# Attention and gated feed-forward on one core: a score product's weight in the merge of two row halves, N/1.2 to N/0.6

## The chip, the cores and the metric

The kernel runs on one NeuronCore of a Trainium2 chip. The metric is the device time of one execution in microseconds, the median of several runs.

## The reference

Attention with a decay term for 8 x 8 heads (sequence 576, head size 64), then a feed-forward block on the 4608 tokens, all in float32:

```python
scores = q @ k.T / 8                      # per head, 576 x 576
cum = cumsum(log(clip(f, 1e-4, 1)))
scores = where(causal, -1e9, scores + cum[:, None] - cum[None, :])
attn = softmax(scores)                    # rows
x = (attn @ v), heads side by side        # 4608 x 512
h = x @ w_in                              # 512 x 2048
out = (h * erf(softplus(h))) @ w_out      # 2048 x 512
```

## The kernel before

There are two stages. In the first, attention, heads are taken in pairs: head 0 of a pair lies in partitions 0 to 63 of the tiles q and k, head 1 in partitions 64 to 127. A matmul that contracts over 64 partitions uses one half of TensorE's rows, so products of head 0 (row half 0) and of head 1 (row half 1) can run side by side. From about 300 us on follows the feed-forward stage (class Moe: line 186 the up products, line 249 the down products), which uses all 128 rows and lies outside the change.

Attention is a loop over steps t = 0 to 67. Two steps make a pair of heads: an even step takes the row blocks 4 and 1, an odd one 3, 2 and 0 (BLOCKS), and the causal width of each block sets the columns of its product (PARTS): 256, 320 and 192 in an even step, 448, 320 and 64 in an odd one, the block of 576 being cut in two. [...] A step t writes, in this order:

- row_halves(t, t - 3): TensorE's score products of step t into two PSUM banks s (one for each head, line 707, and the mask matmuls on the diagonal, line 713), merged with the transposes of step t - 3's probabilities (line 736, into PSUM tiles yz, x and a part of o)
- evacuate(t - 3, 2): ScalarE copies yz (line 799)
- values(t - 4): TensorE's products with v (line 825), over all 128 rows
- run_jobs(t): pieces of weight preparation on VectorE, ScalarE and GpSimd, spread over the steps by a credit for each step
- reduce(t, 0) on VectorE (line 762: adds the decay and takes the extreme, frees the bank of head 0), exps(t, 0) on ScalarE (line 774), invert(t - 1) (reciprocal, VectorE, line 781), normalize(t - 1) on GpSimd (line 788), then reduce(t, 1) and exps(t, 1) for head 1
- evacuate(t - 3) of x and of the part of o on VectorE (line 797), store(t - 4) on VectorE (lines 834 to 838)

Each of the two s banks is used again in the next step, so a product of step t + 1 waits for the reduction of step t of the same head. A transpose in step t waits for normalize of step t - 3, and for the copies that free its PSUM tile.

row_halves merges two lists. List 0 (row half 0) has head 0's products, its masks, and then ten transposes. List 1 (row half 1) has twelve or thirteen transposes first, and then head 1's products and masks. Each item has a cost; each list has a clock. The next item is taken from list 1 if its clock is behind that of list 0, otherwise from list 0, and its cost is added to that list's clock. The costs are 61 for a transpose, 28 for a mask matmul, and for a product of N columns N/1.2. The costs serve only to order the instructions. Steps 1 and 2 list the two halves one after the other (apart=True), step 0 and the steps after 63 have only one kind of work. A product in float32 runs as two passes, each with its own weight load, so it shows as two records.

Of the kernel before, what the change touches and what calls it, by code (L numbers as in the profile page):

```python
# [40 lines left out]
PARTS = [[(512, 4, 320, 576), (192, 4, 0, 320), (0, 1, 0, 192)], [(0, 3, 0, 448), (512, 2, 0, 320), (448, 0, 0, 64)]]  # L41
# [342 lines left out]
def attention_moe(ctx, tc, q2, k2, vp, f, w_in, w_out, out):  # L384
# [283 lines left out]
    with ExitStack() as ph:  # L668
# [31 lines left out]
        def score_work(t):  # L700


            p, half = divmod(t, 2)
            q, k = pairs[p][:2]
            s = [ps_s.tile([P, 1024], F32, name=f"s{t}_{j}", tag="s") for j in range(2)]
            def product(j, at, i, k0, k1):
                nc.tensor.matmul(out=s[j][:, at:at + k1 - k0], lhsT=q[HALF[j], PAD + START[i]:PAD + END[i]],  # L707
                                 rhs=k[HALF[j], k0:k1], start=at in (0, 192, 512) and i != 1, stop=False,
                                 skip_group_check=True)

            def edge(j, i, c):
                to = SCOL[i] + START[i] + 64 * c
                nc.tensor.matmul(out=s[j][:, to:to + 64], lhsT=above[HALF[j], c], rhs=keys[HALF[j]],  # L713
                                 start=False, stop=bool(c), skip_group_check=True)

            raw_scores[t] = s
            probs[t] = wk.tile([P, TCOLS[half]], F32, name=f"pr{t}", tag=f"pr{half}")
            stats[t] = wk.tile([P, 3, 2, len(BLOCKS[half])], F32, name=f"st{t}", tag=f"st{half}")
            return [[((part[3] - part[2]) / 1.2, lambda j=j, part=part: product(j, *part)) for part in PARTS[half]]
                    + [(28, lambda j=j, i=i, c=c: edge(j, i, c)) for i in BLOCKS[half] for c in range(not i, 2)]  # L720
                    for j in range(2)]

# [18 lines left out]
        def row_halves(t, turned=None, apart=False):  # L741

            scored = score_work(t) if t < NH else [[], []]
            moved = [[], []] if turned is None else transpose_work(turned)
            work, clock = [scored[0] + moved[0], moved[1] + scored[1]], [0, 0]
            while any(work):
                h = int(not work[0] or not apart and work[1] and clock[1] < clock[0])
                time, do = work[h].pop(0)
                clock[h] += time
                do()  # L750
# [172 lines left out]
        for t in range(3, NH + 4):  # L923
            p, half = divmod(t, 2)
# [101 lines left out]
```

## Time and profile before

| | before |
|---|---|
| median of 3 runs | 1072.78 us (1072.72 to 1072.9) |
| the profiled execution | 1072.71 us |
| its span, first to last instruction | 1070.8 us |
| granted TensorE clock | 1.000 |
| TensorE busy | 1063.5 us (99%) |
| VectorE, ScalarE, GpSimd busy | 725.4, 779.6, 508.2 us |
| HBM read and written | 113.41 and 39.99 MB |

The busy time of an engine counts any time in which at least one of its instructions runs. PE is TensorE's matmuls, PEld its weight loads, DVE VectorE, ACT ScalarE, POOL GpSimd. Lines in order of time give start and duration in us, engine, line, operation, output and inputs, shape and count; consecutive instructions of the same line are merged into one row under the first one's shape. Ends of matmuls are modelled and include the way through the array, so durations of following matmuls overlap: the distance of starts is the rate.

### The profile page before, as it was taken

To read this page: it belongs to the slowest core of one execution; us is meant where nothing else is said; L and a number is where in the kernel's file an instruction comes from. 1 tells how busy PE (TensorE), PEld (TensorE's weight loads), DVE (VectorE), ACT (ScalarE), POOL (GpSimd) and SP (SyncE) were. 2 spreads that over 40 slices of the span, in tenths; PEclk is the share of its full clock that TensorE was granted. 3 is DMA by queue.
4 is the path that set the end of the run, shared out by engine and by line. 5 is a ranking of instruction groups with operands and counts; after the bars stand their busy time and mean duration, and the time that the engine had idled before them with its cause. 6 is when DMAs were issued, how large, how long until landed. Compare 5 with 4: busy or idle time off the path is not lost.

```text
span 1070.8 us, 22986 instructions
## 1 busy us (share of the span) xinstructions
PE 1063.5 (99%) x8490; PEld 949.9 (89%) x8490; DVE 725.4 (68%) x1701; ACT 779.6 (73%) x1732; POOL 508.2 (47%) x650
## 2 busy tenths in 40 slices
PE   9999999999999999999999999999999999999998
PEld 7888888888898889989999999988988988898996
DVE  6888888988767986776878755646555455655532
ACT  7888888889867787777787776668565665856653
POOL 4578989878534535452633532233143143323313
PEclk9999999999999999999999999999999999999999
DMA  7678887666623152441516154451302213130021
GB/s 267 216 245 267 295 271 267 222 222 222 218 79 132 38 203 84 143 162 61 187 58 219 67 194 190 169 195 55 123 11 79 89 59 118 45 133 1 25 94 59
DMA packets 70366, 154.88 MB, mean 145 GB/s; under 512 B 6960, under 2 KB 19504, under 8 KB 69232
## 3 DMA queue, kind: packets, MB, share of 16 engines
q1 hardware_dynamic: 70256, 153.43, 41.1%
q8 instruction: 67, 1.10, 0.4%
q14 instruction: 43, 0.35, 0.1%
HBM read 113.41 MB, written 39.99 MB: 143 GB/s over the span
## 4 chain that ended last, share of the span: by engine, by line
PE 94%; DVE 3%; ACT 2%; issue 1%; DMA 0%; POOL 0%; DVEq 0%; ACTq 0%; POOLq 0%
PE y L249 35%; PE m L186 31%; PE s L707 11%; PE o L825 9%; PE yz L736 3%; PE x L736 3%; PE s L713 1%; DVE x L127 1%; DVE e L220 0%; ACT L217 0%; ACT e L217 0%; PE o L736 0%; ACT e L214 0%; DMA fr<-in_f_dram 0%; DVE h L210 0%
## 5 line engine op out<-in xcount | busy, mean ns | idle before, releaser
L230 POOL TENSOR_TENSOR gl<-e,gh 128x384 fp32r<-128x384 f32 x192 | 227.0, 1212 | 388.6 <-ACT gh L229 388.6
L186 PE MATMUL m<-x,wi 128*128 128x384 f32 x2016 | 385.6, 337 | 1.0 <-DVE h L210 0.6
L186 PEld LDWEIGHTS m<-x,wi 128*128 128x128 f32 x2016 | 357.3, 188 | 18.9 <-DVE h L210 2.5
L249 PE MATMUL y<-wo,gh 128*128 128x512 f32 x1152 | 359.4, 393 | 0.0
L249 PEld LDWEIGHTS y<-wo,gh 128*128 128x128 f32 x1152 | 214.6, 188 | 34.4
L249 PE MATMUL y<-wo,gl 128*128 128x512 f32 x576 | 227.1, 394 | 0.0
L788 POOL TENSOR_SCALAR pr<-pr,st 128x576 f32<-128x576 f32 (+4 forms) x320 | 173.9, 565 | 67.9 <-DVE st L781 53.5
L707 PE MATMUL s<-k,q 64*128 64x320 f32 (+4 forms) x768 | 195.5, 405 | 0.6 <-PE s L713 0.6
L774 ACT ACTIVATE pr<-pr,st 128x576 f32<-128x576 f32 (+3 forms) x320 | 176.0, 552 | 19.5 <-DVE st L762 16.9
L762 DVE CUSTOM_DVE_ANT_0 pr<-s,c 128x576 f32<-128x576 f32 (+3 forms) x320 | 140.4, 483 | 43.6 <-PE x L736 24.4
L707 PEld LDWEIGHTS s<-k,q 64*128 64x128 f32 x768 | 127.9, 188 | 27.1 <-issue 0.9
L220 DVE TENSOR_TENSOR e<-e,h 128x384 f32<-128x384 f32 x192 | 114.7, 646 | 24.1 <-ACT e L217 24.1
L249 PEld LDWEIGHTS y<-wo,gl 128*128 128x128 f32 x576 | 108.1, 188 | 24.5
L199 ACT COPY sa<-m 128x384 f32<-128x384 f32 x48 | 23.0, 479 | 141.4 <-PE m L186 141.3
L214 ACT ACTIVATE e<-h 128x384 f32<-128x384 f32 x192 | 92.6, 521 | 30.7 <-DVE h L210 22.2
L202 DVE TENSOR_TENSOR sb<-m,sa 128x384 f32<-128x384 f32 x48 | 26.7, 557 | 121.8 <-PE m L186 61.8
L229 ACT CAST gh<-e 128x384 fp32r<-128x384 f32 x192 | 87.9, 511 | 24.7 <-DVE e L220 23.5
L825 PE MATMUL o<-pt,v 128*64 128x128 f32 (+1 forms) x1920 | 102.5, 259 | 0.0
L825 PEld LDWEIGHTS o<-pt,v 128*64 128x64 f32 x1920 | 93.7, 137 | 3.5 <-issue 0.2
L127 DVE TENSOR_TENSOR x<-t,x 128x768 fp32r<-128x768 f32 x77 | 83.8, 1105 | 15.3 <-ACT x L122 15.3
L217 ACT ACTIVATE e<-e 128x384 f32<-128x384 f32 x192 | 84.9, 513 | 0.5
L210 DVE TENSOR_TENSOR h<-m,sb 128x384 f32<-128x384 f32 x96 | 53.1, 553 | 45.8 <-PE m L186 45.8
(112 smaller groups left out, 1237.5 us busy)
## 6 DMA issues: line engine op xcount, KB each, us to landing
v<-in_vp_dram SPq DMA_DIRECT2D x32, 576.0 KB, 4.6
c<-cum_d SPq DMA_DIRECT2D x60, 288.0 KB, 5.9
t<-xt_d SPq DMA_DIRECT2D x44, 384.0 KB, 5.5
q<-in_q_dram SPq DMA_DIRECT2D x32, 320.0 KB, 5.0
k<-in_k_dram SPq DMA_DIRECT2D x32, 288.0 KB, 5.3
xt_d<-xo SPq DMA_DIRECT2D x32, 288.0 KB, 2.3
part_d<-yo SPq DMA_DIRECT2D x36, 256.0 KB, 2.8
yo<-part_d SPq DMA_DIRECT2D x36, 256.0 KB, 4.3
```

The lines of the kernel that those rows point to most:

```text
L127: eng.tensor_tensor(out=x[:, 1, kd], in0=self.src[r][:, kd], in1=x[:, 0, kd].bitcast(F32), op=ALU.subtract)
L186: nc.tensor.matmul(out=ps, lhsT=w[:, wp, ws], rhs=x[:, xp, kd], start=first and kd == 0 and j == 0, stop=kd == 1 and j == 2 and i in (1, 2 ...
L214: self.nc.scalar.activation(out=e, in_=self.h[n, q], func=AF.Softplus)
L220: self.nc.vector.tensor_mul(self.e[n, q], self.e[n, q], self.h.pop((n, q)))
L229: nc.scalar.copy(out=gh, in_=e)
L230: nc.gpsimd.tensor_tensor(out=gl, in0=e, in1=gh.bitcast(F32), op=ALU.subtract)
L249: yield nc.tensor.matmul(out=y[tb], lhsT=g[:, cs], rhs=w[:, f, wp], start=first, stop=last)
L707: nc.tensor.matmul(out=s[j][:, at:at + k1 - k0], lhsT=q[HALF[j], PAD + START[i]:PAD + END[i]], rhs=k[HALF[j], k0:k1], start=at in (0, 192, ...
L762: nc.vector.tensor_tensor_reduce(out=to[:, ::-1] if j else to, in0=score, in1=decay_, scale=-0.125, scalar=BIG, op0=ALU.add, op1=ALU.min, ...
L774: nc.scalar.activation(out=seg, in_=seg, func=AF.Exp, bias=st[:, 0, j, m:m + 1], scale=-1.0, accum_out=st[:, 1, j, m:m + 1])
L788: nc.gpsimd.tensor_scalar(out=seg, in0=seg, scalar1=st[:, 2, j, m:m + 1], scalar2=1.0, op0=ALU.mult, op1=ALU.mult)
L825: nc.tensor.matmul(out=o[h, to:to + 64 * (1 + (a < b))], lhsT=v[:, ch, h], rhs=src, start=m == 0, stop=m == len(parts) - 1, skip_group_che ...
```

## The change

The cost of a score product in the merge goes from N/1.2 to N/0.6. Transposes and masks keep theirs. No instruction is added, removed or altered; the order of TensorE's instructions within row_halves follows from the costs.

```diff
             stats[t] = wk.tile([P, 3, 2, len(BLOCKS[half])], F32, name=f"st{t}", tag=f"st{half}")
-            return [[((part[3] - part[2]) / 1.2, lambda j=j, part=part: product(j, *part)) for part in PARTS[half]]
+            return [[((part[3] - part[2]) / 0.6, lambda j=j, part=part: product(j, *part)) for part in PARTS[half]]
                     + [(28, lambda j=j, i=i, c=c: edge(j, i, c)) for i in BLOCKS[half] for c in range(not i, 2)]
                     for j in range(2)]
```

## The prediction

> **What bounds the kernel now.** I read the page first (engines, the chain that ended last), then the busy time of each engine in the attention stage, then TensorE's and VectorE's instructions in order of time through two steps of that stage.
>
> ```profile
> PE 1063.5 (99%) x8490; PEld 949.9 (89%) x8490; DVE 725.4 (68%) x1701; ACT 779.6 (73%) x1732; POOL 508.2 (47%) x650
> PE 94%; DVE 3%; ACT 2%; issue 1%; DMA 0%; POOL 0%; DVEq 0%; ACTq 0%; POOLq 0%
> PE y L249 35%; PE m L186 31%; PE s L707 11%; PE o L825 9%; PE yz L736 3%; PE x L736 3%; PE s L713 1%; DVE x L127 1%; DVE e L220 0%; ACT L217 0%; ACT e L217 0%; PE o L736 0%; ACT e L214 0%; DMA fr<-in_f_dram 0%; DVE h L210 0%
> ```
>
> TensorE is the chain in both halves of the program. The change touches only the attention stage, up to about 300 us. Twenty-seven pairs of steps (t = 6 to 59), from the start of one even row_halves to another, and two single pairs:
>
> ```profile
> core 0: us, PE busy (x) PEld busy (x) DVE busy (x) ACT busy (x) POOL busy (x), PEclk, DMA share, GB/s
> 30.74:282.83 252.09, 252.09 (x3973) 223.80 (x3969) 218.75 (x838) 216.78 (x673) 207.16 (x355) 1.00 0.74 250
> 114.77:124.11 9.34, 9.34 (x151) 8.30 (x148) 8.37 (x34) 7.64 (x26) 8.46 (x15) 1.00 0.80 231
> 124.11:133.45 9.34, 9.34 (x152) 8.29 (x148) 7.93 (x33) 8.36 (x28) 9.02 (x17) 1.00 1.03 382
> ```
>
> A pair takes 252.09 / 27 = 9.34 us, whatever the others do in it. Their busy time per pair is 8.10 (VectorE), 8.03 (ScalarE), 7.67 (GpSimd), with GpSimd up to 9.02 in a full pair. TensorE is "busy" all the time, but that counts one row half running alone. The two steps, odd (t = 43) then even (t = 44):
>
> ```profile
> 203.35 0.64 PE L707 MATMUL s<-k,q 64*128 64x448 f32 x1
> 203.36 0.64 PE L736 MATMUL yz<-ident,pr 64*128 64x64 f32 x7
> 203.83 0.54 PE L707 MATMUL s<-k,q 64*128 64x448 f32 x1
> 203.84 0.41 PE L736 MATMUL yz<-ident,pr 64*128 64x64 f32 x4
> 204.21 0.43 PE L707 MATMUL s<-k,q 64*128 64x320 f32 x1
> 204.21 0.27 PE L736 MATMUL yz<-ident,pr 64*128 64x64 f32 x1
> 204.48 0.92 PE L707 MATMUL s<-k,q 64*128 64x320 f32 x4
> 204.91 0.31 PE L713 MATMUL s<-keys,above 64*128 64x64 bf16 x5
> 205.06 0.37 PE L736 MATMUL x<-ident,pr 64*128 64x64 f32 x3
> 205.23 0.54 PE L707 MATMUL s<-k,q 64*128 64x448 f32 x1
> ...
> 205.61 0.43 PE L707 MATMUL s<-k,q 64*128 64x320 f32 x1
> ...
> 205.88 0.60 PE L707 MATMUL s<-k,q 64*128 64x320 f32 x3
> 206.31 0.31 PE L713 MATMUL s<-keys,above 64*128 64x64 bf16 x5
> 206.55 1.66 PE L825 MATMUL o<-pt,v 128*64 128x128 f32 x32
> 208.14 0.48 PE L707 MATMUL s<-k,q 64*128 64x256 f32 x1
> 208.15 0.52 PE L736 MATMUL yz<-ident,pr 64*128 64x64 f32 x5
> ...
> 209.54 0.27 PE L736 MATMUL yz<-ident,pr 64*128 64x64 f32 x1
> ...
> 209.66 0.43 PE L707 MATMUL s<-k,q 64*128 64x256 f32 x1
> ...
> 211.22 1.54 PE L825 MATMUL o<-pt,v 128*64 128x128 f32 x28
> ...
> 212.69 0.64 PE L707 MATMUL s<-k,q 64*128 64x448 f32 x1
> ```
>
> ```profile
> L736 PE MATMUL yz<-ident,pr x800: 221/223/274, 17.2 to 315.4; 64*128 64x64 f32 x160
> ```
>
> A product is two records, one for each of two passes. The pass of 448 columns goes from 203.83 to 204.21, 0.38 us; the one of 320 from 204.21 to 204.48, 0.27: a product takes about N/0.6 ns, and the old cost N/1.2 was one pass. The first on an idle half has 0.48 to its second pass, so 0.10 for its weights. Transposes come every 0.062: four from 203.84 last 0.41, less the last one's 0.22 (221 ns above) three intervals of 0.063. The first interval is longer: seven from 203.36 last 0.64, so 0.42 for six, 0.11 and five of 0.062. The cost of 61 is right for them.
>
> Write P for a product of row half 0, T for a transpose, m for a mask matmul, and a prime for half 1. The odd step is listed now: P448 7T' P320 4T' P64 T' 2m P448' 3m 5T P320' 3T ... Each half runs beside the other, ahead of the list, but not far ahead. Four T' start at 203.84, before P320 (204.21), which is listed ahead of them. The twelfth T', behind P64 too, waits until P320 starts. P448' waits much longer: its second pass is at 205.23, so it began at 205.23 - 0.48 = 204.75, while the last T' was through by 204.27. Half 1 stood idle for 0.48, and for 0.1 before that. In the even step the 13th T' is at 209.54 where thirteen need 0.11 + 12 x 0.062 = 0.85, and P256' begins at 209.66, 1.52 after the step's start. Half 1 ends last in both steps, so this idle time is on the path.
>
> **The change part by part.** No instruction is added or removed, on any engine or queue; only the order of TensorE's list in row_halves moves, for t = 3 to 63. Steps 0 to 2 list alike, and after 63 no products are left.
>
> 1. Odd order with N/0.6: P448 12T' P448' P320 P64 4m P320' m 8T P64' 2T 5m'. Half 1 is ready for P448' at 0.11 + 11 x 0.062 = 0.79, and nothing waiting is listed ahead of it: 0.80. From P448' to the values it takes now 206.55 - 204.75 = 1.80. One new hold: P320' is listed behind P64 and four masks, which end at 0.86 + 2 x 0.27 + 0.11 (P64) + 0.20 (0.11 for the first mask's weights, then three of 0.03: five masks last 0.31) = 1.71, where P320' could start at 0.80 + 0.48 + 0.38 = 1.66. I add 0.06. Row_halves: 2.66 for 206.55 - 203.35 = 3.20, that is -0.54. Bounds: 0 (the idle time comes back as other waits) and -0.60.
>
> 2. Even order: P256 7T' P320 6T' P256' P192 P320' 4m 6T P192' 4T 4m'. P256' at 0.86 for 1.52; from there to the values 211.22 - 209.66 = 1.56. So 2.42 for 3.08, -0.66. Bounds 0 and -0.66.
>
> 3. Values are unchanged: 1.59 and 1.47. A pair on TensorE alone is 9.34 - 1.20 = 8.14.
>
> 4. At 8.14 the other engines, at 8.10, 8.03 and 7.67, no longer cover anything for free. What is late next is VectorE:
>
> ```profile
> 205.94 0.62 DVE L762 CUSTOM_DVE_ANT_0 pr<-s,c 128x448 f32<-128x448 f32 x1 [1.34 <-PE x L736]
> ...
> 207.13 0.59 DVE L762 CUSTOM_DVE_ANT_0 pr<-s,c 128x448 f32<-128x448 f32 x1
> ...
> 208.21 0.69 DVE L797 COPY pt<-x 128x512 f32<-128x512 f32 x1
> ...
> 209.47 0.73 DVE L466 SCALAR_TENSOR_TENSOR raw<-raw 128x512 int32<-128x512 int32 x1
> 210.12 0.74 DVE L762 CUSTOM_DVE_ANT_0 pr<-s,c 128x576 f32<-128x576 f32 x1
> ...
> 211.08 0.18 DVE L781 RECIPROCAL st<-st 128x6 f32<-128x6 f32 x1
> ```
>
> The first row shows a second thing: the masks of the first bank ended at 204.91 + 0.31 = 205.22, yet its reduction began at 205.94, just after the second pass of P448' (205.23 + 0.54 = 205.77), which is listed before the last masks. So completions are told in the list's order. With the new order the last mask stands behind P320' in both steps. In the odd step its second pass starts at 2.66 - (206.55 - 205.88) = 1.99 and ends 0.43 later, so the first reduction starts at about 2.5 (now 2.59). In the even step: 0.86 + 0.32 + 0.22 + 0.27 + 0.43 = 2.10.
>
> Follow VectorE from an odd start A, with the even start at A + 2.66 + 1.59 = 4.25 and the next odd at 8.14. Odd reductions: 2.50 to 2.50 + (208.21 - 205.94) = 4.77. P256' needs the bank at 4.25 + 0.86 = 5.11: margin 0.34 (now 209.66 - 208.21 = 1.45). Copies, store and a weight job (210.12 - 208.21 = 1.91) go to 6.68, past the even release at 4.25 + 2.10 = 6.35. Even reductions take 211.08 - 210.12 = 0.96 each and 0.09 for the reciprocal between, 2.0, to 8.68; P448' needs that bank at 8.14 + 0.80 = 8.94: margin 0.26. So a pair with one job in each step fits, and one with a second job of 0.65 in the even step is late by about 0.4, with everything listed behind P' waiting too. Jobs come in batches (VectorE's 8.37 and 7.93 in the neighbouring pairs above); I take 0.4 in four pairs of ten, 0.16 a pair. GpSimd is over 8.14 in its full pairs (9.02, 8.46):
>
> ```profile
> L788 POOL TENSOR_SCALAR pr<-pr,st 128x576 f32<-128x576 f32 x55 | 40.4, 748 | 26.5 <-DVE st L781 26.3
> ...
> L788 POOL TENSOR_SCALAR pr<-pr,st 128x192 f32<-128x192 f32 x54 | 22.4, 428 | 0.0
> ```
>
> The even tile's normalization can start at the reciprocal, about 2.50 + 1.10, takes 2 x 0.75 + 2 x 0.43 = 2.36, and is needed by the transposes at 8.14: some 2 us of slack, in which most of a full pair's excess evens out. I take 0.10 a pair. Bounds of both together: 0, and 1.20, where the whole gain is given back.
>
> The sum: 8.14 + 0.16 + 0.10 = 8.40 a pair, 0.94 less than now. Steps 3 to 63 are 30.5 pairs; I count 29.5, since the first is still filling. 29.5 x 0.94 = 27.7 us. The second stage is TensorE's too and keeps its length, so the gain reaches the end. The profiled execution took 1072.71 us (span 1070.8), the median of the runs is 1072.78, so 1045 for either. Change under 0.2%, about 2 us, can't be told from none.
>
> [...]
>
> **The rivals.**
>
> *TensorE alone sets the pace.* Waits stay near zero: 8.14 to 8.25 a pair, 29.5 x 1.20 = 35 us at most, 1037 to 1041. For it: the margins above, 0.34 and 0.26, are positive. Against: two other engines busy for 8.0 to 8.1 of it, which leaves hardly any room for a late job.
>
> *Another engine becomes the bound.* GpSimd or the weight jobs set 8.7 to 9.2 a pair: gain 4 to 19 us, 1054 to 1068. For it: the row with GpSimd at 9.02 and the DMA share at 1.03. Against: the mean of 7.67.
>
> *Nothing changes.* P' waits for another reason than its place in the list, and starts when it does now: 1072.7. Against it: P448' starts when half 0 moves on, and in the even step the bank of P256' was free 1.45 before it started.
>
> *Starts in list order.* If each matmul waited for the start of the one listed before it, the odd step would run P448 0, second pass 0.48, T' to 1.27, P448' 1.27 and 1.75, P320 1.75 and 2.02, P64 2.29, masks to 2.56, P320' 2.56, T to 3.4, P64' 3.4, masks to 3.75; the present order, counted so, ends at 3.43. That is +0.3, with -0.05 for the even step: +0.25 x 29.5 = +7, 1080. It decides if T' no longer start beside a product's first pass. [...]
>
> *The held release.* The first reduction waits for P320', the two banks arrive nearly together, and P' in the next step waits on VectorE. It is slower once that wait passes the 0.6 won in each step; at 0.75, 59 x 0.15 = +9, 1082. Against: margins of 0.34 and 0.26 before any wait.
>
> **How the numbers follow.** Forecast (8.3 to 8.65 a pair, 1042 to 1053) 0.52; TensorE alone 0.18; another engine 0.17; no change 0.05; list order 0.04; held release 0.04. The first three are faster: 0.87. Same 0.05, slower 0.08. The range, 1037 to 1060, takes in the second and half of the third.
>
> **What would show it.** Pairs of about 8.4 us in the attention stage; the twelve or thirteen T' together within 0.9 of a step's start; P' starting at 0.8 to 0.9; values at about 2.66 and 2.42; VectorE over 95% busy; later stages as long as now. It is wrong if P' still starts at 1.4 to 1.5, or if P' or transposes stand waiting on VectorE or GpSimd for more than 0.3 us a pair.

## The result and the profile after

| | before | after |
|---|---|---|
| median | 1072.84 us (1072.72 to 1073.3) | 1047.46 us (1045.42 to 1049.53) |
| ratio | | 0.9763 (0.9743 to 0.9782) |
| profiled execution | 1072.71 us, span 1070.8 | 1045.42 us, span 1043.5 |

The change made the kernel 25.4 us faster, 2.4%. The forecast was 1045, with a range of 1037 to 1060. The profiled execution is the fastest of four; before, four executions lay within 0.6 us, now within 4.1.

The time came out of the attention stage alone. The last score product starts at 271.7 us after the change and at 299.6 before, so from there to the end of the span it is 771.8 and 771.2 us:

```profile
L707 PE MATMUL s<-k,q x768: 216/429/640, 7.5 to 271.7; 64*128 64x320 f32 x95, 64*128 64x256 f32 x60, 64*128 64x448 f32 x32, 64*128 64x192 f32 x4
```

The same 27 pairs of steps (t = 6 to 59) as the prediction showed, in the busy time of each engine after the change:

```profile
core 0: us, PE busy (x) PEld busy (x) DVE busy (x) ACT busy (x) POOL busy (x), PEclk, DMA share, GB/s
30.28:257.42 227.14, 225.18 (x3973) 211.26 (x3970) 221.44 (x838) 212.73 (x672) 207.65 (x355) 1.00 0.82 276
```

227.14 / 27 = 8.41 us a pair, for 9.34. VectorE is busy for 97% of it, ScalarE 94%, GpSimd 91%. TensorE for the first time has idle time here: 1.96 us.

Two steps that nothing disturbs, an odd one (t = 53) and the even one behind it, TensorE's instructions in order of time (a row stands under its first instruction's shape):

```profile
228.79 0.64 PE L707 MATMUL s<-k,q 64*128 64x448 f32 x1
228.80 0.64 PE L736 MATMUL yz<-ident,pr 64*128 64x64 f32 x7
229.27 0.54 PE L707 MATMUL s<-k,q 64*128 64x448 f32 x1
229.28 0.48 PE L736 MATMUL yz<-ident,pr 64*128 64x64 f32 x5
229.60 0.97 PE L707 MATMUL s<-k,q 64*128 64x448 f32 x6
230.35 0.22 PE L713 MATMUL s<-keys,above 64*128 64x64 bf16 x2
230.41 0.49 PE L707 MATMUL s<-k,q 64*128 64x320 f32 x1
...
230.73 0.43 PE L707 MATMUL s<-k,q 64*128 64x320 f32 x1
...
231.40 1.66 PE L825 MATMUL o<-pt,v 128*64 128x128 f32 x32
232.99 0.48 PE L707 MATMUL s<-k,q 64*128 64x256 f32 x1
...
233.87 0.92 PE L707 MATMUL s<-k,q 64*128 64x256 f32 x5
...
235.43 1.54 PE L825 MATMUL o<-pt,v 128*64 128x128 f32 x28
...
236.90 0.64 PE L707 MATMUL s<-k,q 64*128 64x448 f32 x1
```

All twelve transposes of row half 1 run beside the first product, without a gap between the seventh and the last. Head 1's first product starts right behind them, 229.60 - 228.79 = 0.81 after the step's start where it was 1.40; in the even step 0.88 where it was 1.52. Row_halves takes 2.61 and 2.44 (before 3.20 and 3.08), and the pair 236.90 - 228.79 = 8.11. Most pairs are longer: over the 27 pairs the odd steps lose 3.5 us against their shortest (4.20), a little in each of 18 steps, and the even steps 4.9 against 3.90, of it 3.4 in the four steps 28, 38, 48 and 50.

### The profile page after: what moved, and what is told of

It reads as the page before. It is cut to its first block, busy times and chain, and to the rows that moved or that the text cites. A ratio compares the mean times of both kernels' runs of the same rounds, so it can differ in the third digit from the quotient of the medians.

```text
span 1043.5 us, 22986 instructions
## 1 busy us (share of the span) xinstructions
PE 1032.4 (99%) x8490; PEld 935.2 (90%) x8490; DVE 727.8 (70%) x1701; ACT 775.0 (74%) x1732; POOL 509.2 (49%) x650
## 4 chain that ended last, share of the span: by engine, by line
PE 83%; DVE 6%; POOL 4%; DMA 3%; issue 2%; ACT 2%; SPq 1%; DVEq 0%; POOLq 0%; ACTq 0%
PE y L249 36%; PE m L186 31%; PE o L825 5%; PE s L707 5%; POOL pr L788 3%; PE yz L736 2%; DVE pr L762 2%; PE x L736 2%; PE s L713 1%; DMA c<-cum_d 1%; DMA ta<-xt_d 1%; DVE x L127 1%; DVE pt L797 1%; DMA v<-in_vp_dram 1%; DVE e L220 1%
## 5 line engine op out<-in xcount | busy, mean ns | idle before, releaser
L788 POOL TENSOR_SCALAR pr<-pr,st 128x576 f32<-128x576 f32 (+4 forms) x320 | 181.5, 587 | 39.9 <-DVE st L781 39.2
L707 PE MATMUL s<-k,q 64*128 64x320 f32 (+4 forms) x768 | 163.1, 409 | 2.7 <-issue 1.1
L707 PEld LDWEIGHTS s<-k,q 64*128 64x128 f32 x768 | 109.2, 186 | 15.4 <-issue 2.3
```

The source lines that it names most:

```text
L788: nc.gpsimd.tensor_scalar(out=seg, in0=seg, scalar1=st[:, 2, j, m:m + 1], scalar2=1.0, op0=ALU.mult, op1=ALU.mult)
```

## The experiments

Two theories stood against each other. *Look-ahead*: TensorE starts instructions of one row half ahead of waiting ones of the other, but only past a handful; before, head 1's first product was listed too far behind, and half 1 stood idle. The rival: it pays that the transposes come together, or that both clocks agree with the real durations. Then: what holds the pairs at 8.41 and not 8.11?

| run | what | median us | us a pair | undisturbed odd, even row_halves |
|---|---|---|---|---|
| before | N/1.2 | 1072.84 | 9.34 | 3.20, 3.08 |
| the change | N/0.6 | 1047.46 | 8.41 | 2.61, 2.43 |
| c1_change_again | the same | 1047.75 | 8.45 | 2.61, 2.43 |
| e1_past_masks | N/1.2, one product moved | 1062.02 | 8.99 | 2.85, 3.07 |
| e2_turns_together | N/1.2, transposes moved | 1077.59 | 9.50 | 3.20, 3.24 |
| e3_divisor_05 | N/0.5 | 1045.97 | 8.41 | 2.56, 2.43 |
| e4_masks_first | change + masks listed early | 1044.19 | 8.38 | 2.64, 2.58 |
| e5_odd_masks_first | the same in odd steps only | 1043.79 | 8.36 | 2.64, 2.43 |
| e6_no_words_on_vectore | change, words not converted | 1043.76 | 8.31 | 2.61, 2.43 |
| e7_spread_x_loads | change, x loads spread | 1047.19 | 8.48 | 2.61, 2.43 |
| e8_values_tile_early | change, values tile early | 1045.38 | 8.40 | 2.61, 2.43 |
| e9_combined | e5, e7 and e8 | 1043.00 | 8.34 | 2.64, 2.43 |

Pairs and steps are from one profiled execution each, times from four or five. The change itself was run a second time beside e5 to e7:

> The changed kernel as it is, to stand beside the three below on the same chip: 1045 to 1049, pairs 8.35 to 8.45, undisturbed steps 4.20 and 3.90.

It came to 1047.75 (1046.51 to 1049.38), ratio 0.9765 (0.9751 to 0.978).

### One product past two masks: e1_past_masks

The merge of before, collected in a list first; then

```diff
+            product = order.pop(next(n for n, x in enumerate(order) if x[0] and x[1] not in (28, 61)))
+            order.insert(1 + max(n for n, x in enumerate(order) if x[0] and x[1] == 61), product)
+            for _, _, do in order:
+                do()
```

> The order of before (N/1.2), with one move in each step: head 1's first product goes to directly behind the last transpose of row half 1. In the odd step it passes two masks of 0.03 us each, in the even step one transpose of half 0. Look-ahead theory (half 1 stands idle because its next instruction is listed too many instructions behind waiting ones of half 0): in the odd step the last T' still starts when P320 does, at 0.86, but P448' follows it at 0.93 to 0.97 and no longer at 1.40; P320' moves up by about 0.4; later holds give some back, so the odd row_halves falls from 3.20 to 2.85-2.95. In the even step the 13th T' is held itself behind P192 and masks, so P256' stays near 1.50 and the step at 3.08. Pairs 9.0-9.1, time 1063 to 1068. Rival theory (what pays is that the transposes of half 1 come together, or that both clocks agree with the real durations): nothing of that changes here, moving past 0.06 us of masks is worth at most that, 1071 to 1073.

Measured 1062.02 us, ratio 0.9897 (0.9882 to 0.9911). An odd step of this run:

```profile
205.51 0.64 PE L707 MATMUL s<-k,q 64*128 64x448 f32 x1
...
206.37 0.27 PE L736 MATMUL yz<-ident,pr 64*128 64x64 f32 x1
206.49 0.97 PE L707 MATMUL s<-k,q 64*128 64x448 f32 x5
...
208.36 1.66 PE L831 MATMUL o<-pt,v 128*64 128x128 f32 x32
```

The twelfth transpose is held as before, to 0.86. The product follows it at 0.98 and not at 1.40, and the step takes 2.85 and not 3.20. Passing two masks that together run for 0.06 us won 0.35: no duration explains that, the place in the list does. Even steps stayed as they were (3.07 for 3.08), since their last transpose is itself held, to 1.40. The time is 1 us under the range expected.

### Transposes together, product left behind: e2_turns_together

```diff
+            turns = [x for x in order if x[0] and x[1] == 61]
+            rest = [x for x in order if not (x[0] and x[1] == 61)]
+            order = rest[:1] + turns + rest[1:]
```

> The order of before (N/1.2), with one move in each step: all twelve or thirteen transposes of row half 1 go directly behind head 0's first product, as in the change in the odd step; everything else stays, so head 1's first product stays behind head 0's products and two masks (odd) or all masks and a transpose (even). Look-ahead theory: the transposes end at 0.8, half 1 then stands idle until the product comes into reach, at about 1.40 (odd, as before) and 1.55 to 1.65 (even, now behind 0.10 more of waiting). Steps 3.20 and 3.10 to 3.25, time 1072 to 1077. Rival theory (together is what pays): 1045 to 1055.

Measured 1077.59 us, ratio 1.0042 (1.0026 to 1.0059): slower. Row half 1 has all its transposes early, as in the change, and gains nothing:

```profile
206.44 0.64 PE L707 MATMUL s<-k,q 64*128 64x448 f32 x1
206.45 0.65 PE L736 MATMUL yz<-ident,pr 64*128 64x64 f32 x7
206.92 0.54 PE L707 MATMUL s<-k,q 64*128 64x448 f32 x1
206.94 0.48 PE L736 MATMUL yz<-ident,pr 64*128 64x64 f32 x5
207.30 1.18 PE L707 MATMUL s<-k,q 64*128 64x320 f32 x5
...
208.32 0.54 PE L707 MATMUL s<-k,q 64*128 64x448 f32 x1
...
209.64 1.66 PE L832 MATMUL o<-pt,v 128*64 128x128 f32 x32
```

The transposes are through at about 207.2, but P448' has its second pass at 208.32, so it began at 208.32 - 0.48 = 207.84, 1.40 after the step's start: to the hundredth where it was before. The rival theory falls.

In even steps P256' went from 1.52 to 1.63. Here head 0's own products are late: P320 is now listed behind thirteen transposes of the other half and starts 0.63 after the step's start, where it was 0.54 before.

```profile
211.23 0.48 PE L707 MATMUL s<-k,q 64*128 64x256 f32 x1
...
211.86 0.53 PE L707 MATMUL s<-k,q 64*128 64x320 f32 x1
...
212.86 0.48 PE L707 MATMUL s<-k,q 64*128 64x256 f32 x1
```

How far is the reach? Count each pass as a weight load and a matmul (before has 768 of each for its 384 products). In the prediction's odd step the held transpose starts when one matmul and P64's two loads and two matmuls wait ahead of it, five; a moment earlier, behind seven, it does not. P448' in e1 also starts behind five. So the reach lies at five or six waiting instructions, three of them matmuls. The traces bear this out: with every record of steps 8 to 57 put beside its place in the list, in before, e1, e2, the change, e3 and e4, no matmul starts while more than three matmuls listed ahead of it wait, and in before ten in each pair of steps start behind exactly three. P320 at 0.63 above starts behind exactly three as well, all transposes.

### The hold of P320': e3_divisor_05

```diff
-            return [[((part[3] - part[2]) / 0.6, ...
+            return [[((part[3] - part[2]) / 0.5, ...
```

> The changed kernel with N/0.5 for N/0.6: in the odd step P320' is listed before the masks of head 0 and not behind four of them; in the even step only transposes are dealt out otherwise. Look-ahead theory: the hold of P320' (0.06 to 0.1) goes, the undisturbed odd row_halves falls from 2.61 to 2.50, the even one stays at 2.43. If TensorE sets the pace in most steps, 20 of 28 odd steps gain 0.1, 1044 to 1046 beside 1047.5 for the change; if the other engines do, no difference (1047 to 1049). First VectorE reduction about 0.1 earlier in the odd step.

1045.97 us (1044.89 to 1047.79), ratio 0.9749 (0.9734 to 0.9763); the intervals of this and the change overlap, so the time does not decide, though it lies in the range expected for a TensorE that sets the pace. Odd row_halves has a least value of 2.56 and a median of 2.60 (steps 5 to 63), not 2.50. The pair is the same 8.41, but step 28 took 6.20 in this execution and 4.96 in the change's, which hides 0.05 a pair. More speed for TensorE alone brings at most about that.

### Completions in the list's order: e4_masks_first and e5_odd_masks_first

```diff
                 h = int(not work[0] or not apart and work[1] and clock[1] < clock[0])
+                if work[0] and work[0][0][0] == 28:
+                    h = 0
```

(in e5 with `t % 2 and` ahead of the condition)

> The changed kernel, but head 0's masks are listed as soon as its products are through, so ahead of P320' of head 1 in both steps. The last mask then stands behind P448' or P256' only. If completions are told in the list's order, the first VectorE reduction starts in an odd step at about 1.9 and not 2.4 after the step's start, in an even step at 1.7 and not 2.05, where VectorE is free by then. Price: P320' is held behind the masks, +0.03 in the odd and +0.1 to 0.16 in the even undisturbed step (2.64 and 2.55 to 2.59). If late banks come from that held release, the disturbed odd steps (2.89) fall to 2.65 and the time is 1043 to 1047; if they come from VectorE's backlog of weight jobs, the price stands alone: 29 x 0.17 = 5, 1050 to 1053.

1044.19 us, ratio 0.9734 (0.9719 to 0.9749). VectorE's first reduction in an odd step, first in the change (t = 53, step from 228.79), then in this run (t = 53, from 227.42; the row of the first product stands with it):

```profile
231.21 0.62 DVE L762 CUSTOM_DVE_ANT_0 pr<-s,c 128x448 f32<-128x448 f32 x1 [0.31 <-PE s L713]
```

```profile
227.42 0.64 PE L707 MATMUL s<-k,q 64*128 64x448 f32 x1
...
228.98 0.25 PE L713 MATMUL s<-keys,above 64*128 64x64 bf16 x3
...
229.32 0.62 DVE L764 CUSTOM_DVE_ANT_0 pr<-s,c 128x448 f32<-128x448 f32 x1
```

2.42 after the step's start in the change, where VectorE had waited 0.31 for it, and 1.90 here, straight behind its previous job. The masks themselves run at the same time in both (230.35 - 228.79 = 1.56 in the change, 228.98 - 227.42 = 1.56 here). The second pass of P320', listed before the last mask in the change, ends at 230.73 + 0.43 = 231.16, and the reduction starts at 231.21. So in these runs the end of a bank's masks is told after the products listed before the last of them. The odd steps of 2.89 are gone but for one at 2.92. The price is as expected, 0.03 and 0.15 in the undisturbed steps, 5 us in all; that the time still fell by 3 us puts the worth of the early release, as an estimate by that count, at about 8 us. The 3 us are at the edge of the noise: the ratio's interval just overlaps that of the change (0.9743 to 0.9782) and not that of its second run (0.9751 to 0.978).

> Head 0's masks ahead of P320' in odd steps only; even steps as in the change. Held-release theory: odd steps keep what the run with masks first in both gave them (4.23 in nearly every step, no 4.48), even steps go back to 3.90 undisturbed where they were 4.05: pairs about 8.2 to 8.3, time 1040 to 1043. If the even steps need the early release as much as the odd ones (VectorE then runs late there), the 0.15 won is lost again in waits: 1044 to 1047.

1043.79 us, ratio 0.9728 (0.9711 to 0.9744). This is not told apart from e4, and lies between the two ranges expected. Undisturbed even steps went back to 3.90, but steps 26, 28, 38 and 48 took 0.6 to 1.5 longer: the pair is 8.36, not 8.2 to 8.3. The waits that its trace names on TensorE are mostly for GpSimd (2.8 us together; no other sums to more than 0.4).

### VectorE's backlog: e6_no_words_on_vectore

The first weight blocks are not converted here (VectorE's four passes over their words are left out).

```diff
+        normal = low_bits = lowest_bits = join = lambda m: None
```

> The changed kernel without VectorE's four passes over the weights' words in the attention stage (lines 456, 461, 466 and 471; the first weight blocks are then not converted). Backlog theory: about 28 us of VectorE work in steps 5 to 47 goes, 1.3 a pair; banks are reduced in time, odd steps of 4.48 become 4.20 to 4.25, pairs 8.15 to 8.25 with what is left of GpSimd's and the transfers' waits: 1040 to 1043. If the remaining 0.31 a pair over 8.10 comes from GpSimd or transfers alone: 1046 to 1049.

1043.76 us, ratio 0.9727 (0.9712 to 0.9741), 4.0 us under the change on the same chip:

```profile
30.16:254.46 224.30, 220.71 (x3973) 208.30 (x3969) 193.75 (x798) 211.37 (x672) 194.47 (x355) 1.00 0.82 279
```

VectorE is busy for 28 us less in these 27 pairs, and a pair falls from 8.45 to 8.31 (224.30 / 27), less than expected; the time lies just above the range. More than half of what stands over 8.10 is left, most of it in five even steps (18, 28, 40, 48 and 50); the odd steps lose 0.6 us in all where the second run of the change loses 2.6. GpSimd's busy time falls too, from 207.65 to 194.47 with the same 355 instructions, so the run does not tell what VectorE's passes cost directly from what they cost through GpSimd.

### Transfers: e7_spread_x_loads and e8_values_tile_early

```diff
-            job("x", j, SP, 0, lambda j=j: load_first(j), [], 24)
+            job("x", j, SP, 0, lambda j=j: load_first(j), [], 24 + 2 * j)
```

> The changed kernel, but the eight 192 KB loads of the first x (tiles ta and tb) go out two at a time in steps 24, 26, 28 and 30, not all in step 24. In the change's trace they hold the transfer queue from 109.75 to 117.2, the values tile of the next pair is issued at 118.44, lands 6.16 later, and step 28 takes 4.96 instead of 3.90. If that queue is its cause, step 28 falls to 3.9 to 4.1 and the time by 0.8 to 1.1; if the burst of transfers itself is, it stays within 0.3.

1047.19 us (1046.88 to 1048.14) beside 1047.75 (1046.51 to 1049.38) on the same chip: not told apart. Step 28 did fall, from 4.96 to 4.10, as expected if the queue was its cause. That is not shown: the step also took 4.20 in e4, which leaves these loads alone, and 6.20 in e3. What is shown, by the chain of waits in the change, is the late tile of v and the work that waited for it:

```profile
118.44 6.16 DMA v<-in_vp_dram
```

```profile
124.64 1.54 PE L825 MATMUL o<-pt,v 128*64 128x128 f32 x28 [0.26 <-DMA v<-in_vp_dram]
```

Other even steps of this execution took 1.0 to 1.6 us too long (18, 38, 48 and 62).

```diff
-            if half == 0 and t <= NH:
-                load_values(p - 1)
...
             if added:
                 values(t - 4)
+            if half == 1 and t < NH:
+                load_values(p)
```

> The changed kernel, but the values tile of the next pair is requested in the odd step, behind values(t - 4) and ahead of the store, and no longer at the head of the even step behind that store. The request no longer waits for VectorE's store copies, so it goes out 2 to 3 us earlier. If late values tiles (0.85 and 0.58 in steps 28 and 26 of the second run of the change, 0.84 in step 38 of the run with spread loads) are what is left beside VectorE's backlog and what makes runs of one kernel differ by 4 us, the values in even steps start without such gaps, the time falls to 1044.5 to 1046.5 and the spread of runs under 2 us. If the sporadic stalls without a visible wait (1.0 to 1.4, one or two a run) make the spread, it stays at 2 to 4 us and the time at 1046 to 1048.

1045.38 us (1045.0 to 1046.81), ratio 0.9736 (0.9722 to 0.9749); the change had 0.9765 (0.9751 to 0.978) in its second run. 2.4 us faster, at the edge of the noise: the two intervals do not touch, but that of the change's first run (0.9743 to 0.9782) overlaps. No wait for v stands in its list of waits any more. In the changed kernel the request stood behind the store of the previous pair, which waits for VectorE (27 waits between 20 and 280 us of the change, 135.7 us together), and a pair that is 10% shorter leaves it less slack. The five executions lie within 1.8 us, those of e7 within 1.3, so the closer spread is not shown to be this edit's doing.

One kind of pause was not tested. One to five times in an execution of the changed kernel and its variants TensorE stands still for 0.3 to 1.2 us, with no wait to be seen. In c1_change_again, by the chain of waits:

```profile
173.84 0.06 PE s L707
173.90 1.23 issue
175.13 0.27 PE x L736
```

"Issue" is time in which the engine waited for nothing that the profile shows. The traces hold a lead. Packets of 16 KB of the DMA kind "instruction" land in the attention stage of the change on average every 7.0 us: 38 between 20 and 285 us, in which TensorE has 9123 matmuls and weight loads, 240 to a packet. In this run one lands at 173.78, 1.35 before the pause ends; of the 16 such pauses (over 0.25 us) in the attention stage of the change, its second run and e3 to e9, 15 end 1.2 to 1.6 us behind such a landing. Before has no such pause. What TensorE waits for there is not shown, and no run tests it.

### Together: e9_combined

> Odd steps with head 0's masks first, the values tile requested early, the first x in four pairs of loads: what each of the three took away should add up as far as it was of different steps. 1043.8 (masks first in odd steps) less 0.5 to 2.5 for late transfers: 1041 to 1043.5. If VectorE's backlog holds whatever the transfers leave, no better than 1043.5 to 1044.

1043.00 us (1042.61 to 1044.65), ratio 0.9716 (0.9703 to 0.973): the fastest run, 4.5 us below the change, within the range and near its upper end.

## Why the prediction was right, point by point

**Steps 1 and 2, the two row_halves.** 2.66 and 2.42 were forecast, 2.61 and 2.44 measured; P' at 0.80 and 0.86, measured 0.81 and 0.88. The working from starts and from what is listed ahead held to 0.05, and e1 and e2 showed that the mechanism behind it, and not the durations or the grouping, makes the gain. The hold of P320' behind the masks exists but is worth 0.05 (0.06 was added), by the least value of the run with N/0.5, which expected 0.11.

**Step 3**, 8.14 for TensorE alone: 8.11 in undisturbed pairs.

**Step 4, the completion in the list's order.** First reduction in an odd step at 2.50: 2.42 where VectorE waits for it. e4 confirms the reading by moving it to 1.90. In the even step VectorE's own backlog decides, as forecast.

**Step 4, what the others cost.** 0.26 a pair was taken, 0.16 for VectorE's jobs and 0.10 for GpSimd; measured are 8.41 - 8.11 = 0.30 in the first profile, as much as the prediction allowed before it would call itself wrong. Without the weight words' passes the time falls by 4.0 us, 4.0 / 29.5 = 0.14 a pair, close to the 0.16; GpSimd's share of it is not known. The loss has another shape than forecast: not 0.4 in four odd steps of ten, but up to 0.28 in 17 of 27 and 0.43 in one, 0.13 on average. The other term is not shown where it was put. GpSimd was not tested alone, but the early request of the values tile is worth some 2.4 us, 0.08 a pair, and the prediction had no term for transfers, although the DMA share of 1.03 stood in its rows, nor for the pauses. So it is partly luck that the sum came within 0.01 of the first profile's 8.41; the second run's profile has 8.45. Late transfers may be most of the 2.4 us between the 1045 forecast and the median: e8, with the early request, is at 1045.4.

**The rivals.** Starts in list order fell with the transposes and products above, which run ahead of products listed before them. TensorE alone did not come true: VectorE is busy for 97%, and with less for it to do (e6) or an earlier release (e4) the time falls. The held release was real: it took back some 8 us (by e4's count), but the wait seen in seven odd steps, 0.28, stays under the 0.6 that would have decided. Only single steps reach that: step 50, behind two VectorE jobs of 1.88 together, took 0.93 too long, 0.38 of it a pause, and is back at 4.05 in e4. "Another engine becomes the bound" did not: the mean of 8.41 stays below the 8.7 from which that rival counted, though a single pair like that of steps 28 and 29 (4.96 + 4.20) is above it. "Nothing changes" fell with the result, and e1 shows that the place in the list is what P' waited for.

## What to carry to other kernels

When two halves of TensorE's rows work on lists of their own, list each half's next instruction so that, when it could start, no more than three matmuls listed ahead of it still wait (the reach in the six runs above): durations in the merge need to be true only so far that neither half runs out of reach. Where a result is released in the list's order, as here (at 2.42, and by 1.90 with a product of the other half listed later), put the instruction that completes a bank ahead of long products of the other half, if the consumer is the next bound. After such a gain look at once for requests in the transfer queue that wait behind a store: slack counted in steps shrinks with the steps.

## What the runs showed of the hardware

- A matmul of one row half started before matmuls of the other half that were listed ahead of it, past up to three waiting matmuls (five or six instructions with their weight loads), and past no more in any of 50 steps of six runs; a product listed two masks (0.06 us) later started 0.42 later.
- Completions across the halves were told in the list's order: masks that started at 1.56 were told at 2.42 behind a product of the other half, and by 1.90 with that product listed later.
- Executions of the change spread over 4.1 and 2.9 us, those of its variants over 0.7 to 2.9, those of before over 0.2 to 2.4 in the comparisons of these experiments. What makes the difference was not found.
- 15 of 16 pauses of TensorE without a visible wait ended 1.2 to 1.6 us after a 16 KB packet of the kind "instruction" had landed; the cause is not tested.
